# A fused attention and phase-MLP kernel: two groups' phase step in halves, and the whole written-out order replaced

## The chip, the cores and the metric

The kernel runs on one core of a Trainium2 chip. The metric is the device time of one execution in microseconds. Before the change it is 210.47 us, the median of three runs (208.16 to 210.56). The profiled execution took 208.09 us, with a span of 206.3 us from the first instruction to the last; all times of single instructions are from that one.

## What is computed

Two layers, one after the other. The first is attention inside chunks of 64 positions, for 8 batches, 8 heads, 576 positions and a head width of 64. The second works on x, the attention's result with the heads side by side (8 x 576 x 512):

```
scores = scale * q_c @ k_c^T          (per chunk of 64)
x      = softmax(scores) @ v_c
theta  = x @ w_theta
zr, zi = x * cos(theta), x * sin(theta)
y      = w_tok_r @ zr + w_tok_i @ zi  (over the 576 positions of a batch)
u      = x + y
out    = u + relu(u @ w_ch)
```

Inputs and output are fp32; q, k, v and the weights become fp16 on their way into SBUF (theta's weights on the chip), and products accumulate in fp32.

## The kernel before

**Tiles and groups.** The batches are taken in four pairs, numbered 0 to 3. A pair has 2 x 576 rows, nine tiles of 128 rows, numbered 0 to 8. Five groups of tiles pass through the attention together: A (tiles 0, 1) and B (2, 3) of the pair's first batch, C (5, 6) and D (7, 8) of its second, and M, the middle tile 4, whose two halves of 64 rows come from the two batches.

**The order.** There is no scheduler. The string `ORDER` (lines 18 to 66) lists some 650 steps, and the loop at line 589 emits them one after the other. Each engine takes its own instructions in that order; semaphores between engines follow from the tiles. A step is written kind, then pair and group (or pair and tile), then on TensorE steps the PSUM slot. `H.1C.2` is theta of pair 1, group C, into slot 2. The text writes `H.1C` for it. Whoever moves a step in the list moves it on one engine's queue only, and everything behind it on that queue follows.

**The steps of a group**, with the engine that does each:

- `q`, `k`, `v` (lines 170 to 185): loads from HBM, two DMAs each, issued by GpSimd, which converts to fp16. `lw` loads the token weights, `lc` the channel weights, `lt` (SyncE) theta's weights.
- `T`: 32 transposes of q and k on TensorE (16 for M), and `tq` (VectorE) or `tqa` (ScalarE) to copy them from PSUM.
- `S`: scores; `e`: exponentials on ScalarE; `V0`, `V1`: times v, four heads each, with the sum as a 65th column; `v0`, `v1`: normalization on VectorE, which gives x.
- `X` with `x` (ScalarE) or `xv` (VectorE): x transposed on TensorE and copied; or `Xd` (line 388): one DMA transpose on SyncE instead of both.
- `H` (line 399): theta, eight matmuls on 512 columns for a group of two tiles; `g` (line 415): cos and sin on ScalarE; `z` (line 430): the two products on VectorE. For M, `zm` (line 446) moves two halves by DMA.
- `TW` with `twd`: the token weights transposed, once in the kernel, in four pieces.

**The steps of a tile:** `Y` (line 456): nine matmuls with the token weights (in the first pair also in three pieces `Ya`, `Yb`, `Yc`, for tiles 0 to 3); it needs z of both groups of its batch and of M. `y`: u = x + y on VectorE. `U` with `ua` or `uv`: u transposed on TensorE and copied; or `Ud` (line 497): a DMA transpose on SyncE. `W`: four matmuls with the channel weights; `w`: relu and sum; `st`, `sa`: the stores, from SyncE's queue and in the last pair also from ScalarE's.

**Fillers.** `D` (line 155) is one matmul on a blank tile whose result nobody reads. There are 60; they keep TensorE busy while it would wait.

**Buffers that matter.** PSUM has three slots of two banks ("wide") and two of one bank ("thin", for Y, U, W and fillers). cos and sin have three buffers each, q and k eight, the transposed x three, the transposed u five. SyncE's queue is in order as well: a DMA transpose that waits for its data holds up every store and transpose behind it.

Of the kernel before, what the change touches and what calls it, by code (L numbers as in the profile page):

```python
# [10 lines left out]
FP16 = mybir.dt.float16  # L11
# [4 lines left out]


ORDER = """
lt.00 ones.00 D.00.0 D.00.1 D.00.0 D.00.1 D.00.0 D.00.1 D.00.0 q.0M lw.00 q.0B lw.01
D.00.1 D.00.0 init.00 D.00.1 D.00.0 D.00.1 D.00.0 D.00.1 D.00.0 new.00 D.00.1 D.00.0  # L20
k.0M q.0A D.00.1 TW.00.0 D.00.0 v.0M D.00.1 D.00.0 D.00.1 D.00.0 D.00.1 TW.01.1 new.10
T.0M.2 k.0B tq.0M D.00.0 q.0C D.00.1 S.0M.2 twd.00 k.0A D.00.0 D.00.1 v.0B v.0A e.0M
ct.00 D.00.0 D.00.1 D.00.0 D.00.1 D.00.0 lw.02 V1.0M.0 D.00.1 D.00.0 D.00.1 T.0B.2 k.0C
D.00.0 q.0D D.00.1 twd.01 D.00.0 D.00.1 V0.0M.1 v1.0M D.00.0 v0.0M v.0C D.00.1 D.00.0
tqa.0B X.0M.0 D.00.1 S.0B.1 e.0B T.0A.2 D.00.0 lw.03 xv.0M H.0M.0 q.1M D.00.1 D.00.0
k.0D tq.0A S.0A.1 e.0A V1.0B.2 q.1C D.00.1 V0.0A.1 v1.0B v0.0A D.00.0 D.00.1 V0.0B.2
q.1D v0.0B D.00.0 V1.0A.1 D.00.1 X.0B.2 v1.0A X.0A.1 g.0M T.0C.0 x.0B k.1M xv.0A D.00.0
H.0A.1 g.0A z.0M D.00.1 H.0B.2 g.0B tq.0C z.0A S.0C.0 z.0B TW.03.1 Ya.00.0 v.0D zm.0M
TW.02.2 Yb.00 e.0C Yc.00 lc.00 twd.02 T.0D.0 V0.0C.2 twd.03 V1.0C.1 y.00 Ya.02.1 U.00.0
Yb.02 Yc.02 v1.0C v.1M v0.0C y.02 X.0C.1 T.1M.2 tq.1M tqa.0D S.0D.0 k.1C q.1B ua.00  # L30
Ya.03.0 Yb.03 U.02.1 e.0D xv.0C H.0C.2 q.2M V0.0D.0 v0.0D ua.02 V1.0D.1 v1.0D k.1D q.1A
Yc.03 y.03 S.1M.0 e.1M W.02.1 v.1C g.0C V1.1M.1 X.0D.0 W.00.0 xv.0D H.0D.0 k.2M w.00
k.1B w.02 v.1D v1.1M T.1C.2 v.2M q.2C Ya.01.0 Yb.01 U.03.1 g.0D v.1B V0.1M.1 z.0C tq.1C
q.3M z.0D st.00 T.1D.0 S.1C.2 ua.03 Yc.01 v0.1M k.1A y.01 Y.05.1 y.05 U.01.0 T.2M.1
tqa.1D tq.2M uv.01 S.1D.0 e.1C W.03.1 U.05.0 T.1B.2 e.1D uv.05 V0.1C.1 w.03 V1.1C.0
Y.06.0 W.01.1 st.02 v.1A v1.1C v0.1C q.2A y.06 V1.1D.0 tqa.1B S.2M.2 v1.1D V0.1D.1
Y.08.0 w.01 U.06.1 e.2M v0.1D S.1B.2 y.08 X.1D.0 ua.06 xv.1D X.1C.1 e.1B Y.07.0 T.1A.0
V1.1B.2 y.07 q.2B x.1C X.1M.1 tqa.1A xv.1M v1.1B Y.04.1 S.1A.1 st.03 q.3C k.2C q.2D y.04
V1.2M.2 H.1M.0 new.20 v1.2M U.08.0 e.1A W.05.1 w.05 V0.2M.2 ua.08 U.07.0 g.1M k.2B v0.2M
H.1D.1 k.3C uv.07 U.04.1 g.1D z.1M H.1C.2 ua.04 V1.1A.0 v1.1A V0.1A.1 v0.1A g.1C W.06.0  # L40
W.04.1 st.01 q.3D X.2M.0 x.2M X.1A.1 w.06 T.2C.2 xv.1A T.2B.0 w.04 z.1D tqa.2C z.1C
W.08.0 w.08 H.1A.1 V0.1B.2 tqa.2B g.1A st.05 k.2D zm.1M v.3D k.2A k.3M q.3A W.07.1 w.07
Y.16.0 H.2M.0 st.06 D.00.1 v0.1B y.16 v.2C v.2B X.1B.1 k.3D v.3A xv.1B T.2D.2 g.2M
U.16.0 st.04 uv.16 H.1B.0 st.08 st.07 W.16.1 q.3B z.2M tq.2D w.16 Y.18.0 S.2C.1 S.2D.2
g.1B e.2D z.1A T.3M.0 Y.15.1 S.2B.2 z.1B e.2C y.18 y.15 Y.10.0 tqa.3M y.10 V1.2C.1
T.2A.0 v.2A e.2B V1.2B.2 D.00.1 U.10.0 v1.2C Y.13.1 ua.10 v1.2B U.18.0 V0.2C.1 tq.2A
S.2A.2 uv.18 T.3D.0 Y.12.0 y.13 U.13.1 tq.3D v0.2C V0.2B.0 k.3A e.2A V0.2A.2 S.3D.1 v.2D
y.12 ua.13 U.12.0 v0.2B W.10.1 w.10 k.3B ua.12 W.13.0 w.13 W.18.1 st.16 w.18 Y.14.0
T.3C.0 v.3M e.3D T.3A.1 v0.2A U.15.1 V1.2D.2 y.14 st.10 v1.2D Y.11.0 tqa.3C V0.2D.0
st.18 v0.2D ua.15 T.3B.2 tq.3A st.13 Y.17.1 X.2C.0 y.11 S.3A.1 tqa.3B xv.2C S.3B.2 e.3B  # L50
W.15.0 V1.2A.0 v1.2A Xd.2A y.17 Ud.14 H.2C.2 e.3A V1.3A.1 X.2D.0 new.30 Ud.11 xv.2D g.2C
W.12.1 H.2D.0 g.2D Xd.2B v1.3A w.15 W.14.0 w.12 z.2C Ud.17 v.3B z.2D v.3C H.2A.1 W.11.1
st.12 w.14 H.2B.2 zm.2M w.11 V1.3D.0 g.2A st.14 z.2A st.15 v1.3D V0.3A.1 v0.3A Y.27.0
st.11 Y.25.1 V0.3D.0 g.2B y.27 Ud.27 S.3C.2 e.3C z.2B y.25 S.3M.1 v0.3D W.17.0 Ud.25
w.17 Y.26.1 e.3M V0.3M.0 st.17 V1.3M.2 V1.3B.1 y.26 v1.3B Xd.3A v0.3M v1.3M Xd.3M Xd.3D
Y.24.0 V0.3B.1 y.24 Ud.24 V0.3C.0 v0.3C V1.3C.2 v1.3C W.25.1 w.25 st.25 Y.23.0 y.23
W.27.1 w.27 Ud.26 Ud.23 st.27 Y.28.0 W.24.1 w.24 H.3A.0 st.24 H.3M.2 Xd.3C W.26.1 y.28
v0.3B Y.22.0 Xd.3B Ud.28 w.26 g.3M y.22 st.26 Y.20.1 y.20 Y.21.0 z.3M Ud.20 y.21 H.3B.1
W.28.1 w.28 g.3B Ud.22 W.23.0 zm.3M W.22.1 w.23 w.22 g.3A z.3A H.3C.2 st.23 H.3D.1 st.28
st.22 Ud.21 W.20.0 g.3C z.3B Y.30.1 w.20 y.30 g.3D Ud.30 Y.32.0 z.3D y.32 Ud.32 Y.33.1  # L60
Y.31.0 z.3C y.33 Y.35.1 st.20 y.31 y.35 Ud.31 W.30.0 w.30 W.32.1 w.32 W.21.0 Ud.33 sa.30
st.32 sa.32 Ud.35 w.21 Y.38.1 y.38 st.21 W.31.0 st.30 w.31 Ud.38 Y.34.1 y.34 st.31
W.33.0 Ud.34 w.33 st.33 Y.36.1 y.36 Ud.36 Y.37.0 y.37 W.35.1 w.35 Ud.37 W.34.0 sa.33
sa.31 w.34 st.35 st.34 sa.35 W.38.1 W.36.0 w.38 w.36 sa.34 st.38 W.37.1 D.00.0 D.00.0
w.37 sa.37 st.36 sa.36 D.00.1 sa.38 st.37 D.00.0
""".split()


# [1 line left out]
def kernel(  # L70
# [11 lines left out]
    nc = tc.nc  # L82
    B, H, S, D = q.shape
    DM = H * D
    CH = 64
    P = 128
    NDB = DM // P
# [10 lines left out]
    GROUPS = {  # L98
        "M": (MID, None, KT * P),
        "A": (0, 0, 0),  # L100
        "B": (2, 0, GT),
        "C": (5, 1, 0),
        "D": (7, 1, GT),
    }
# [14 lines left out]
    tmp = ctx.enter_context(tc.tile_pool(name="tmp", bufs=3))  # L119
# [3 lines left out]
    def psum2(name, slot, dtype=FP32):  # L123
        n = 1024 if dtype == FP32 else 2048
        return wide.tile([P, n], dtype, name=name, tag=f"wide{slot}")

    def psum1(name, slot, dtype=FP32):
        n = 512 if dtype == FP32 else 1024
        return thin.tile([P, n], dtype, name=name, tag=f"thin{slot}")
# [18 lines left out]
    st = {p: {} for p in range(NP)}  # L148
# [230 lines left out]
    def x_copy(p, g, copy):  # L379
        n = 1 if g == "M" else 2  # L380
        psv = st[p].pop(("ps_xT", g))
        xT = tmp.tile([P, 2 * NDB, P], FP16, name="xT")
        st[p]["xT", g] = xT
        copy(  # L384
            out=xT[:, 0 : n * NDB].rearrange("p a (r c) -> p r a c", r=2), in_=psv
        )
# [9 lines left out]

    def theta(p, g, slot):
        j0, bb, s0 = GROUPS[g]  # L400
        n = 1 if bb is None else 2
        xT = st[p].pop(("xT", g))
        ps = psum2("ps_theta", slot)
        for j in range(n):
            for db in range(NDB):
                nc.tensor.matmul(  # L406
                    ps[:, j * DM : j * DM + DM],
                    xT[:, j * NDB + db, :],
                    wtheta16[:, db, :],
                    start=(db == 0),  # L410
                    stop=(db == NDB - 1),
                )
        st[p]["ps_theta", g] = ps

    def trig(p, g):
        n = 1 if g == "M" else 2
        ps = st[p].pop(("ps_theta", g))
        cos = tmp.tile([P, 2, DM], FP16, name="cos16")
        sin = tmp.tile([P, 2, DM], FP16, name="sin16")
        st[p]["trig", g] = cos, sin  # L420
        pin = ps[:, 0 : n * DM]
        nc.scalar.activation(  # L422
            out=cos[:, 0:n].rearrange("p a e -> p (a e)"), in_=pin,
            func=AF.Sin, bias=pihalf, scale=1.0,
        )
        nc.scalar.activation(  # L426
            out=sin[:, 0:n].rearrange("p a e -> p (a e)"), in_=pin, func=AF.Sin
        )

    def phase(p, g):  # L430
        j0, bb, s0 = GROUPS[g]
        cos, sin = st[p].pop(("trig", g))
        x, zr, zi = st[p]["x"], st[p]["zr"], st[p]["zi"]
        if bb is not None:
            nc.vector.tensor_mul(zr[:, j0 : j0 + 2], x[:, j0 : j0 + 2], cos)
            nc.vector.tensor_mul(zi[:, j0 : j0 + 2], x[:, j0 : j0 + 2], sin)
            return
        lo, hi = half
        t = tmp.tile([P, DM], FP16, name="zmid")
        nc.vector.tensor_mul(t[lo], x[lo, j0], sin[lo, 0])  # L440
        nc.vector.tensor_mul(t[hi], x[hi, j0], cos[hi, 0])
        st[p]["zmid"] = t
        nc.vector.tensor_mul(zr[lo, j0], x[lo, j0], cos[lo, 0])
        nc.vector.tensor_mul(zi[hi, j0], x[hi, j0], sin[hi, 0])

# [82 lines left out]
    def store(p, j, queues):  # L528
# [38 lines left out]
        "x": lambda p, g: x_copy(p, g, nc.scalar.copy),  # L567
        "xv": lambda p, g: x_copy(p, g, nc.vector.tensor_copy),
        "H": theta,
        "g": trig,  # L570
        "z": phase,
        "zm": mid_move,
        "D": idle,
        "Y": y,
# [13 lines left out]
    with tc.manual_schedule():  # L588
        for step in ORDER:
            kind, at, *slot = step.split(".")  # L590
            g = int(at[1]) if at[1].isdigit() else at[1]
# [31 lines left out]
```

The softmax here doesn't subtract the row's maximum and nothing guards it: scores larger than these inputs give would overflow.

## Time and profile before

| engine | busy of the 206.3 us | share |
|---|---|---|
| TensorE matmuls | 191.7 (19.1 of it fillers) | 93% |
| VectorE | 127.5 | 62% |
| GpSimd (loads) | 106.3 | 51% |
| ScalarE | 95.0 | 46% |

| DMA | count | size | us to landing, median |
|---|---|---|---|
| loads of q, k, v by GpSimd | 96 | 128 KB | 5.8 to 6.4 |
| the same, middle tile | 24 | 64 KB | 6.2 to 6.3 |
| stores | 72 | 128 KB | 2.5 to 2.6 |
| DMA transposes of u | 21 | 128 x 512 | 2.5 |
| DMA transposes of x | 7 | 128 x 1024 (one half as wide) | 3.4 |

A busy TensorE is not one at work to its peak: ends of matmuls are modelled, and a matmul on 512 columns is listed at about 380 ns while the next starts 216 ns later. So the text takes start-to-start times for TensorE's steps. Idle time of the other engines matters only where TensorE waits for them. The loads go on until GpSimd's last issue at 111 us and land until 119.8 us; the DMA engines move 147 to 220 GB/s in nearly every slice of that time.

### The profile page before, as it was taken

To read this page: it belongs to the slowest core of one execution; us is meant where nothing else is said; L and a number is where in the kernel's file an instruction comes from. 1 tells how busy PE (TensorE), PEld (TensorE's weight loads), DVE (VectorE), ACT (ScalarE), POOL (GpSimd) and SP (SyncE) were. 2 spreads that over 40 slices of the span, in tenths; PEclk is the share of its full clock that TensorE was granted. 3 is DMA by queue.
4 is the path that set the end of the run, shared out by engine and by line. 5 is a ranking of instruction groups with operands and counts; after the bars stand their busy time and mean duration, and the time that the engine had idled before them with its cause. 6 is when DMAs were issued, how large, how long until landed. Compare 5 with 4: busy or idle time off the path is not lost.

```text
span 206.3 us, 6334 instructions
## 1 busy us (share of the span) xinstructions
PE 191.7 (93%) x2770; PEld 95.3 (46%) x2770; DVE 127.5 (62%) x234; ACT 95.0 (46%) x94; POOL 106.3 (51%) x133
## 2 busy tenths in 40 slices
PE   7779789999989999999999999799999989999991
PEld 2334445554654654554465554344544434444430
DVE  0032488857948557969588665867845645844470
ACT  2016468837954679956725349486002077000000
POOL 7989999988999999967988200000000000000000
PEclk9999999999999999999999999999999999999998
DMA  5999999999999999999999922975867859247665
GB/s 191 181 158 154 161 163 177 147 173 154 197 159 180 186 155 180 180 220 198 187 156 147 186 89 53 128 171 113 129 118 151 166 126 157 51 102 176 160 166 134
DMA packets 139546, 31.88 MB, mean 154 GB/s; under 512 B 132224, under 2 KB 134400, under 8 KB 139520
## 3 DMA queue, kind: packets, MB, share of 16 engines
q0 software_dynamic: 114288, 16.02, 116.5%
q1 hardware_dynamic: 24512, 14.30, 30.9%
q10 hardware_dynamic: 720, 1.18, 2.2%
q8 instruction: 21, 0.34, 0.7%
q14 instruction: 5, 0.04, 0.1%
HBM read 33.06 MB, written 9.44 MB: 206 GB/s over the span
## 4 chain that ended last, share of the span: by engine, by line
PE 60%; POOL 17%; DMA 14%; issue 2%; ACT 2%; DVE 1%; SPq 0%; DVEq 0%; ACTq 0%; POOLq 0%
PE ps_y L475 29%; PE ps_uw L512 12%; POOL qk L174 12%; PE ps_theta L406 9%; POOL v L182 4%; DMA wnat<-in_moe_w_tok_i_dram 3%; DMA wch<-in_moe_w_ch_dram 3%; DMA uT<-u 3%; DMA qk<-in_k_dram 3%; PE ps_qkT L262 3%; PE ps_x L341 3%; PE ps_sT L308 2%; PE ps_uT L492 1%; DMA out_dram<-o 1%; POOL wnat L192 1%
## 5 line engine op out<-in xcount | busy, mean ns | idle before, releaser
L475 PEld LDWEIGHTS <-wT 128*128 128x128 f16 (+1 forms) x360 | 30.5, 100 | 34.4 <-issue 1.2
L475 PE MATMUL ps_y<-zr,wT 128*128 128x512 f16 (+1 forms) x180 | 44.3, 381 | 0.0
L475 PE MATMUL ps_y<-zi,wT 128*128 128x512 f16 (+1 forms) x180 | 41.9, 379 | 0.0
L483 DVE TENSOR_TENSOR u<-ps_y,x 128x512 f16<-128x512 f32 x36 | 24.8, 690 | 21.6 <-PE ps_y L475 21.3
L512 PE MATMUL ps_uw<-wch,uT 128*128 128x512 f16 x144 | 35.8, 380 | 2.2 <-DMA uT<-u 2.2
L174 POOL DMA_DIRECT2D qk<-in_q_dram x40 | 34.3, 881 | 3.7 <-issue 1.4
L182 POOL DMA_DIRECT2D v<-in_v_dram x40 | 34.2, 878 | 3.0 <-DMA qk<-in_k_dram 1.1
L422 ACT ACTIVATE cos<-ps_theta,pihalf 128x1024 f16<-128x1024 f32 (+1 forms) x20 | 20.6, 1031 | 31.7 <-PE ps_theta L406 30.2
L174 POOL DMA_DIRECT2D qk<-in_k_dram x40 | 34.3, 879 | 1.7 <-DMA wnat<-in_moe_w_tok_i_dram 0.6
L406 PE MATMUL ps_theta<-wtheta,xT 128*128 128x512 f16 x144 | 34.0, 379 | 0.0
L521 DVE SCALAR_TENSOR_TENSOR o<-ps_uw,u 128x512 f32<-128x512 f32 x36 | 24.6, 689 | 15.0 <-PE ps_uw L512 14.6
L321 ACT ACTIVATE eT<-ps_sT 128x1024 f16<-128x1024 f32 (+1 forms) x20 | 18.5, 938 | 30.0 <-PE ps_sT L308 28.7
L354 DVE TENSOR_TENSOR x<-ps_x,recip 128x512 f16<-128x512 f32 (+1 forms) x40 | 25.5, 638 | 1.4
L512 PEld LDWEIGHTS <-uT 128*128 128x128 f16 x144 | 12.8, 97 | 18.1 <-DMA uT<-u 3.6
L287 ACT COPY qkT<-ps_qkT 128x2048 f16<-128x2048 f16 x9 | 16.7, 1867 | 9.7 <-PE ps_qkT L262 9.5
L406 PEld LDWEIGHTS <-xT 128*128 128x128 f16 x144 | 13.4, 98 | 16.0 <-DVE xT L384 1.1
L157 PE MATMUL ps_idle<-blank 128*128 128x512 f16 x60 | 19.1, 432 | 1.4 <-DVE pihalf L145 1.2
L426 ACT ACTIVATE sin<-ps_theta 128x1024 f16<-128x1024 f32 (+1 forms) x20 | 18.7, 935 | 0.0
L353 DVE RECIPROCAL recip<-ps_x 128x8 f32<-128x8 f32 (+1 forms) x40 | 7.9, 196 | 11.8 <-PE ps_x L341 11.5
L262 PE MATMUL ps_qkT<-id,qk 64*128 64x64 f16 x576 | 12.5, 191 | 1.8 <-DMA qk<-in_k_dram 1.7
L262 PEld LDWEIGHTS <-qk 64*128 64x128 f16 x576 | 10.0, 95 | 5.0 <-DMA qk<-in_k_dram 2.2
L341 PE MATMUL ps_x<-v,eT 64*64 64x65 f16 x576 | 11.1, 196 | 1.1 <-ACT eT L321 0.7
(42 smaller groups left out, 133.5 us busy)
## 6 DMA issues: line engine op xcount, KB each, us to landing
out_dram<-o SPq DMA_DIRECT2D x63, 128.0 KB, 2.5
qk<-in_q_dram POOLq DMA_DIRECT2D x32, 128.0 KB, 6.4
qk<-in_k_dram POOLq DMA_DIRECT2D x32, 128.0 KB, 6.4
v<-in_v_dram POOLq DMA_DIRECT2D x32, 128.0 KB, 5.8
out_dram<-o ACTq DMA_DIRECT2D x9, 128.0 KB, 2.6
theta<-in_moe_w_theta_dram SPq DMA_DIRECT2D x1, 1024.0 KB, 5.3
wnat<-in_moe_w_tok_r_dram POOLq DMA_DIRECT2D x2, 288.0 KB, 6.3
wnat<-in_moe_w_tok_i_dram POOLq DMA_DIRECT2D x2, 288.0 KB, 6.9
```

Of the source, the lines that this page charges most:

```text
L157: nc.tensor.matmul(ps, blank[:, 0:P], blank, start=True, stop=True)
L174: nc.gpsimd.dma_start(nats[p, g][rows, which, r], (q, k)[which][b, :, t0 : t0 + n, :].rearrange("h s d -> s h d"),)
L182: nc.gpsimd.dma_start(v16[rows, slot + r, :, 0:D], v[b, :, t0 : t0 + n, :].rearrange("h s d -> s h d"),)
L262: nc.tensor.transpose(psv[:, r, w, e, j, :], t[half[r], w, j, 2 * e : 2 * e + 2, :].rearrange("s h d -> s (h d)"), id16[half[r], half[r]],)
L354: nc.vector.tensor_tensor(out=st[p]["x"][:, j0 : j0 + n, f * NE * D : (f + 1) * NE * D].rearrange("p c (h d) -> p c h d", h=NE), in0=psv[: ...
L406: nc.tensor.matmul(ps[:, j * DM : j * DM + DM], xT[:, j * NDB + db, :], wtheta16[:, db, :], start=(db == 0), stop=(db == NDB - 1),)
L422: nc.scalar.activation(out=cos[:, 0:n].rearrange("p a e -> p (a e)"), in_=pin, func=AF.Sin, bias=pihalf, scale=1.0,)
L426: nc.scalar.activation(out=sin[:, 0:n].rearrange("p a e -> p (a e)"), in_=pin, func=AF.Sin)
L475: nc.tensor.matmul(ps[rows], wT[:, kt, cols], z[:, jz, :], start=(kt == 0), stop=(kt == 2 * KT),)
L483: nc.vector.tensor_tensor(out=u, in0=st[p].pop(("ps_y", j))[:, 0:DM], in1=st[p]["x"][:, j], op=ALU.add)
L512: nc.tensor.matmul(ps, uT[:, db * P : db * P + P], wch16[:, db, :], start=(db == 0), stop=(db == NDB - 1),)
L521: nc.vector.scalar_tensor_tensor(out=o, in0=st[p].pop(("ps_uw", j)), scalar=0.0, in1=u, op0=ALU.max, op1=ALU.add)
```

## The change

Two things are done. First, theta, cos/sin and the products can be done for one tile of a group: `Ha`, `ga`, `za` for the first and `Hb`, `gb`, `zb` for the second. The half theta goes into a thin PSUM slot of one bank. The new order uses the halves for groups A and B of pair 0 alone, the first two whole groups. There the chain from theta over cos/sin to z is at the start of everything that follows, and a half can go on while the other is still computed.

Second, `ORDER` is replaced whole, with the aim of keeping DMA transposes clear of the loads. The list has the same loads, matmuls and stores. It has 60 fillers as well, but 36 of them stand ahead of the first `TW` (18 before) and 11 at the end (4 before). Of the copies after `T`, 15 are VectorE's and 5 ScalarE's (10 and 10 before); of those after `X`, 3 are VectorE's and 10 ScalarE's (10 and 3 before). One more tile's u is transposed by DMA (22, 21 before) and one less on TensorE.

The diff of the functions, and the head of the list (the rest of it is as new as this part):

```diff
 ORDER = """
-lt.00 ones.00 D.00.0 D.00.1 D.00.0 D.00.1 D.00.0 D.00.1 D.00.0 q.0M lw.00 q.0B lw.01
-D.00.1 D.00.0 init.00 D.00.1 D.00.0 D.00.1 D.00.0 D.00.1 D.00.0 new.00 D.00.1 D.00.0
-k.0M q.0A D.00.1 TW.00.0 D.00.0 v.0M D.00.1 D.00.0 D.00.1 D.00.0 D.00.1 TW.01.1 new.10
...
-H.0A.1 g.0A z.0M D.00.1 H.0B.2 g.0B tq.0C z.0A S.0C.0 z.0B TW.03.1 Ya.00.0 v.0D zm.0M
-TW.02.2 Yb.00 e.0C Yc.00 lc.00 twd.02 T.0D.0 V0.0C.2 twd.03 V1.0C.1 y.00 Ya.02.1 U.00.0
...
+v.0M v.0A q.0C D.00.1 D.00.0 D.00.1 D.00.0 D.00.1 D.00.0 T.0M.1 tq.0M S.0M.2 e.0M TW.01.1
+D.00.0 T.0B.2 twd.00 D.00.1 D.00.0 v.0B D.00.1 T.0A.0 D.00.0 q.0D lw.02 twd.01 D.00.1
+V0.0M.1 tq.0A tqa.0B v0.0M S.0A.2 e.0A V1.0M.0 S.0B.1 v1.0M D.00.0 e.0B X.0M.2 V0.0A.0
+k.0C V1.0A.1 x.0M H.0M.2 new.10 v0.0A v1.0A X.0A.0 xv.0A V1.0B.1 Ha.0A.1 v1.0B V0.0B.0
+g.0M ga.0A v0.0B lw.03 k.0D z.0M Hb.0A.0 v.0C q.1C X.0B.1 TW.02.2 twd.02 gb.0A T.0C.0
+x.0B q.1D Ha.0B.1 zm.0M Hb.0B.0 tq.0C zb.0A za.0A v.0D TW.03.1 ga.0B gb.0B S.0C.2 twd.03
+q.1M T.0D.0 e.0C lc.00 Ya.02.1 zb.0B Ya.03.0 k.1D Yb.02 Yb.03 za.0B Yc.03 y.03 Yc.02
...
 """.split()
...
+    def tiles_of(g, t):
+        j0, bb, s0 = GROUPS[g]
+        return j0 + (t or 0), 1 if bb is None or t is not None else 2
+
+    def theta(p, g, slot, t=None):
+        n = tiles_of(g, t)[1]
+        xT = st[p]["xT", g]
+        ps = psum2("ps_theta", slot) if t is None else psum1("ps_theta1", slot)
...
-                    xT[:, j * NDB + db, :],
+                    xT[:, (j + (t or 0)) * NDB + db, :],
...
-    def phase(p, g):
-        j0, bb, s0 = GROUPS[g]
-        cos, sin = st[p].pop(("trig", g))
+    def phase(p, g, t=None):
+        bb = GROUPS[g][1]
+        j0, n = tiles_of(g, t)
+        cos, sin = st[p].pop(("trig", g, t))
...
-            nc.vector.tensor_mul(zr[:, j0 : j0 + 2], x[:, j0 : j0 + 2], cos)
-            nc.vector.tensor_mul(zi[:, j0 : j0 + 2], x[:, j0 : j0 + 2], sin)
+            nc.vector.tensor_mul(zr[:, j0 : j0 + n], x[:, j0 : j0 + n], cos[:, 0:n])
+            nc.vector.tensor_mul(zi[:, j0 : j0 + n], x[:, j0 : j0 + n], sin[:, 0:n])
...
+        "Ha": lambda p, g, slot: theta(p, g, slot, 0),
+        "Hb": lambda p, g, slot: theta(p, g, slot, 1),
+        "ga": lambda p, g: trig(p, g, 0),
+        "gb": lambda p, g: trig(p, g, 1),
+        "za": lambda p, g: phase(p, g, 0),
+        "zb": lambda p, g: phase(p, g, 1),
```

The loads begin, with the number of DMAs of each in brackets, before: q.0M (2), lw.00 (1), q.0B (2), lw.01 (1), k.0M, q.0A, v.0M, k.0B, q.0C, k.0A, v.0B, v.0A, lw.02, k.0C, q.0D (2 each); after: q.0M (2), q.0B (2), lw.00 (1), q.0A (2), k.0M (2), lw.01 (1), k.0B, k.0A, v.0M, v.0A, q.0C, v.0B, q.0D, lw.02, k.0C (2 each).

## The prediction

> **What bounds the kernel now.** I read the busy time by stages first, for all work and then for the filler matmuls of line 157 alone (columns: stage, its length, busy time of PE, PEld, DVE, ACT and POOL, granted clock, DMA share, GB/s; the second answer has PE and PEld only).
>
> ```profile
> 0.00:34.00 34.00, 28.04 (x458) 13.31 (x460) 13.22 (x28) 13.38 (x13) 31.61 (x45) 1.00 1.89 170
> 34.00:100.00 66.00, 64.73 (x1204) 35.15 (x1202) 48.90 (x94) 47.37 (x48) 60.88 (x73) 1.00 2.23 177
> 126.00:132.00 6.00, 4.62 (x51) 1.93 (x49) 5.05 (x10) 4.98 (x5) 0.00 (x0) 1.00 0.81 98
> 132.00:200.00 68.00, 67.21 (x491) 30.33 (x490) 42.07 (x74) 17.46 (x19) 0.00 (x0) 1.00 0.68 136
> ```
> ```profile
> 0.00:34.00 34.00, 16.98 (x54) 5.24 (x54) 1.00 1.89 170
> ```
>
> From 34 us on TensorE is full: 64.73 of 66 and 67.21 of 68. In the first 34 it is not: of 28.04 busy, 16.98 are fillers. So a better order can gain in two places only, the start and the few holes later. The timeline of TensorE shows those (start, length, work, and in brackets the idle time before it and what ended it):
>
> ```profile
> 25.49 0.32 PE L341 MATMUL ps_x<-v,eT 64*64 64x65 f16 x16 [0.69 <-ACT eT L321]
> 28.53 0.41 PE L372 MATMUL ps_xT<-id,x 64*128 64x64 f16 x16 [0.43 <-DVE x L354]
> 29.73 1.90 PE L406 MATMUL ps_theta<-wtheta,xT 128*128 128x512 f16 x8
> 31.68 1.89 PE L406 MATMUL ps_theta<-wtheta,xT 128*128 128x512 f16 x8
> 59.27 0.29 PE L262 MATMUL ps_qkT<-id,qk 64*128 64x64 f16 x7 [0.88 <-DMA qk<-in_k_dram]
> 131.56 1.04 PE L512 MATMUL ps_uw<-wch,uT 128*128 128x512 f16 x4 [1.38 <-DMA uT<-u]
> 168.30 1.04 PE L512 MATMUL ps_uw<-wch,uT 128*128 128x512 f16 x4 [0.79 <-DMA uT<-u]
> ```
>
> The start hangs on loads and on the chain behind them; TensorE has dense real work from H.0B, at 31.68. Later a load ends one hole (59) and DMA transposes end two (131, 168). With small ones (0.25 at 35.7, 0.10 at 53.6, 0.44 at 104) the holes sum to 3.9 us. SyncE's queue shows why 131 happened:
>
> ```profile
> 126.17 1.34 SPq L393 DMA_TRANSPOSE xT<-x  x1
> 127.63 2.78 SPq L500 DMA_TRANSPOSE uT<-u  x2
> 130.51 1.26 SPq L393 DMA_TRANSPOSE xT<-x  x1
> 131.86 1.24 SPq L500 DMA_TRANSPOSE uT<-u  x1
> ```
>
> Ud.14, wanted by W.14, was queued behind Xd.2A, which waited for the normalization of group A. The last loads were issued by
>
> ```profile
> 111.42 3.52 POOL L182 DMA_DIRECT2D v<-in_v_dram  x4 [0.16 <-issue]
> ```
>
> and landed at 119.8, so even before the change no transpose met a load; it is the queue and the short distance that cost.
>
> **What the skill says.** The Trainium skill, "DMA: Bandwidth & Descriptors", Issuing engines are not separate DMA queues: DMAs of all issuers share the same 16 engines and interleave. The trace agrees: the 64 KB middle moves took up to 5.7 us to land while loads ran and 1.9 at the end. "TensorE: Matmul & The Clock Gate", What's actually happening: the array drops to half clock after about an idle window of 3.4 us, and needs as much work to come back. The trace agrees for the start: 18 fillers took 6.62 us (368 ns each), six later ones 1.47 (245); its clock column, 1.00 throughout, does not show it. "ScalarE: Activation LUTs", What ACT_TABLE_LOAD costs: a load takes 1283 ns; here ten of 1283. In the new order Exp and Sin alternate as often (ten loads), so this costs nothing.
>
> **The change, part by part.**
>
> Halves. Theta of 0A and 0B in two pieces of four matmuls is the same TensorE work (2 x 0.865 for 1.73). ScalarE: a pair cos and sin on 1024 columns is 1117 + 1021 ns, on 512 it is 687 + 589, so halves cost 2 x 1.28 - 2.14 = 0.42 us more per group. VectorE: no half tile is in the trace; bounds are 0.34 (half of the 684 ns of a 1024-column product) and 0.42 (64 rows x 512 columns). I take 0.42: four make 1.68 against 1.37, 0.3 us more per group. What it buys: cos of the first half starts 0.87 us sooner.
>
> Copies. Over the run five q/k transposes' copies go from ScalarE (1.87) to VectorE (1.22) and seven xT copies the other way (0.69 to 1.02): VectorE +6.1 - 4.8, ScalarE -9.4 + 7.1. Both are below 65% busy, so nothing on the path in sum. I laid the new VectorE and ScalarE sequences against TensorE's with the durations of the rows: in the worst stretch (37 to 60 us) VectorE is nearly full, and Y.06 and S.1C come 0.43 and 0.24 us late. I count 0.4.
>
> Start. Loads keep their pace (about 0.88 us an issue, 6 us to land), so the n-th landing moves little. v.0A becomes load 17 and 18, where k.0A was (TensorE waited for that until 21.98), instead of landing at 24.67. k.0C becomes 27 and 28, where q.0D landed at 29.74 and 30.61. In the new TensorE order T.0C stands ahead of Ha.0B and everything behind it waits, so T.0C ends at 30.61 + 0.5 = 31.1 and Ha.0B starts there. Before it, A's chain fits: x.0B is copied by 29.6 (X.0B at 27.5, ScalarE busy with both cos/sin pairs of A until 28.6, then 1.02). Start of dense work: 31.1 against 31.68, gain 0.58. At this point TW.02 is done already (0.87 of work that before lay behind H.0B); two later fillers (0.43) and one U transpose (0.27: transposes by DMA go from 21 to 22) are gone. Gain 1.57. Summed by rows (Y 1.98 each, W 0.90, H 1.73, T 0.57, S 0.375, V 0.25, X 0.29, U 0.27), the work from this point to the last W is 163.6 us before and 162.0 after. Before took 168.4 (31.68 to 200.1): 3.9 of holes and 0.9 of small steps between groups, which I leave as they are. After Ya and Yb, Yc.03 needs za.0B: ga.0B from 32.0, gb.0B from 34.0 (it takes the cos/sin buffer that za.0A frees, behind tq.0C and zb.0A on VectorE) to 35.2, then two products pairs to 36.9; TensorE is there at 36.4, and its fourth matmul first reads the last of them. Late by 0.1.
>
> Loads later. With TensorE dense from 31.1 I set each group's first use against the landing of the same load number: T.1D 1.0 us to spare, T.1C 0.3, T.1B 0.1, V0.1C 0.5 late, T.1A 0.2 late, T.3A 0.4 late, all of pair 2 two to twenty us early. One shift of 0.5 serves all. Before, the same table is late by up to 2.5 (T.2M, V0.2A) and the holes made up for it.
>
> DMA transposes. From the producer's end on TensorE to the consumer's start the new order leaves Ud.14 30 us (before 15), Ud.11 14, Xd.2A 9.1 (before 7.4), Xd.3A 6.7, Ud.22 18.5 (before 8.1). Ready plus 0.8 us, issue and landing take 3.4 to 5.7, so the holes at 131 and 168 (2.2 us) go. Ud.34 at the end has 3.6, as Ud.37 had 3.5. I keep 0.3 for one that queues.
>
> Fillers. 36 of the 60 now stand ahead of TW.00: 12 slow and 24 at 0.22 end at 11.6 us, when the first token weights have long landed (9.05 before, about 9.9 after), but k.0M lands at 13 to 14.5 and hides this. The 11 at the end run beside the last store (2.5 us). No cost.
>
> Sum: end of TensorE 200.1 - 0.58 - 1.57 - 3.87 + (0.5 loads, 0.4 VectorE, 0.1 Yc, 0.3 transposes, 0.5 for what the table does not see) = 195.9. The tail of 6.2 us (last W, store, end) stays. Span 202.1 of 206.3, ratio 0.980; of 210.47 this is **206.2**.
>
> **Rivals.** (A) New waits take the place of the old: the new order has as little room between steps (x.1B and z of pair 0's C and D 0.04 us, y.02 0.07), so it loses the same 4.8 us over its sum: 31.1 + 162.0 + 4.8 = 197.9, gain 2.2, 208.2 us. For it: before, eleven links had under 0.5 us to spare, now thirteen. Against: the big holes were transposes, which now have room. (B) Slower: between 12 and 31 us TensorE loses its fillers, and waits for T.0C ahead of ready work. If it cools, the five theta pieces and the first transposes run at half pace, up to 5 us; or k.0C lands 2 to 3 us later and all behind it with it: 200.1 - 2.2 - 2 + 5 and more, 212 us. Against: gaps there are 0.5 to 1.5 us, well under the window. (C) No new waits at all: 31.1 + 162.0 + 0.9 = 194.0, 204.2 us.
>
> **How the numbers follow.** Forecast 0.45, A 0.30, B 0.13, C 0.12. A quarter of all is the forecast's lower half and with C and a little of A makes 0.42 for faster than 206.3; B's upper part and accidents make 0.13 for slower; 0.45 lies between. Range 203.2 to 211.0: from below C to most of B.
>
> **What would show it.** T.0C ends near 31.1, waiting for k.0C, and Ha.0B starts at once; matmuls of 220 ns there (not 430) rule out cooling. No hole over 0.5 us from a uT or xT landing; q/k/v landings end holes of at most 0.5 near 59 and 106. Last W ends near 196. It is wrong if k.0C lands after 32, if fillers' absence shows as slow matmuls, or if holes from VectorE in 37 to 60 exceed 1 us.

## The result and the profile after

The changed kernel took 202.98 us (median of 4 runs, 202.68 to 203.27), the kernel before 209.37 in the same session (4 runs, 208.16 to 210.56). The ratio is 0.9695, with a 95% interval of 0.9618 to 0.9772: faster by 3%. Two of the four runs before lie near 210.5; against the usual time of that kernel (208.1 to 208.8, see the first experiment) the gain is nearer 5 us than 6.4. The ratios leave out executions over 1.5% above the fastest of the same kernel, so a ratio can differ a little from the quotient of the medians. The profiled executions last 201.2 and 206.3 us. The forecast of 206.2 was 3.2 us too high, and the result lies just below its range (203.2 to 211.0).

By stages, all work of the kernel after (columns as in the prediction: stage, its length, PE, PEld, DVE, ACT, POOL, clock, DMA share, GB/s):

```profile
0.00:34.00 34.00, 29.23 (x521) 14.92 (x521) 15.17 (x34) 16.62 (x20) 32.37 (x45) 1.00 1.91 172
34.00:100.00 66.00, 64.94 (x1206) 34.73 (x1207) 49.21 (x93) 40.85 (x44) 59.85 (x73) 1.00 2.23 173
126.00:132.00 6.00, 6.00 (x151) 3.13 (x138) 5.08 (x12) 2.35 (x3) 0.00 (x0) 1.00 0.35 68
132.00:196.00 64.00, 61.33 (x386) 26.67 (x385) 39.70 (x67) 15.14 (x16) 0.00 (x0) 1.00 0.72 144
```

and the fillers of line 157 alone (PE and PEld):

```profile
0.00:34.00 34.00, 14.42 (x49) 5.11 (x49) 1.00 1.91 172
```

In the first 34 us TensorE does 14.8 us of real work (29.23 - 14.42) where before it did 11.1. The hole at 131 is gone (6.00 of 6). From 132 on the picture is worse than before: 2.67 us idle of 64, against 0.79 of 68.

TensorE's timeline of the kernel after shows the start and the new holes:

```profile
29.77 0.38 PE L262 MATMUL ps_qkT<-id,qk 64*128 64x64 f16 x14 [0.35 <-DMA qk<-in_k_dram]
30.08 1.90 PE L410 MATMUL ps_theta<-wtheta,xT 128*128 128x512 f16 x8
34.08 0.38 PE L262 MATMUL ps_qkT<-id,qk 64*128 64x64 f16 x14 [0.52 <-DMA qk<-in_k_dram]
60.55 0.32 PE L341 MATMUL ps_x<-v,eT 64*64 64x65 f16 x14 [0.78 <-DMA v<-in_v_dram]
140.79 1.90 PE L410 MATMUL ps_theta<-wtheta,xT 128*128 128x512 f16 x8 [0.45 <-DMA xT<-x]
159.25 1.90 PE L517 MATMUL ps_uw<-wch,uT 128*128 128x512 f16 x8 [1.07 <-DMA uT<-u]
171.82 1.04 PE L517 MATMUL ps_uw<-wch,uT 128*128 128x512 f16 x4 [0.54 <-DMA uT<-u]
195.65 1.04 PE L517 MATMUL ps_uw<-wch,uT 128*128 128x512 f16 x4 [0.45 <-DMA uT<-u]
```

T.0C waits for k.0C (landed 29.73), Ha.0B starts at 30.08. From there on, with 0.19 at 69 (V0.1B) and 0.17 at W.33, the holes sum to 4.17 us: three of loads (1.49: T.0D, V0.1C, V0.1B) and five of DMA transposes (2.68: H.3A, W.21, W.22, W.33, W.34). SyncE's queue shows how the two largest holes of transposes arise:

```profile
155.27 1.34 SPq L393 DMA_TRANSPOSE xT<-x  x1
156.70 1.21 SPq L505 DMA_TRANSPOSE uT<-u  x1
158.01 2.46 SPq L543 DMA_DIRECT2D out_dram<-o  x4
160.52 1.35 SPq L393 DMA_TRANSPOSE xT<-x  x1
161.97 1.18 SPq L543 DMA_DIRECT2D out_dram<-o  x2
163.25 1.25 SPq L505 DMA_TRANSPOSE uT<-u  x1
164.59 0.54 SPq L454 DMA_DIRECT2D zr<-zmid  x1
165.23 0.55 SPq L455 DMA_DIRECT2D zi<-zmid  x1
165.82 1.23 SPq L543 DMA_DIRECT2D out_dram<-o  x2
167.15 1.25 SPq L505 DMA_TRANSPOSE uT<-u  x1
```

Ud.21 (156.70) stands behind Xd.3D (155.27) and lands at 159.2, when W.21 starts. Ud.22 (167.15) stands behind Xd.3C, a store, Ud.23, two middle moves and another store, and lands at 171.8.

The tail, from the last W's end (200.1 and 196.5, its start plus the 0.87 us that a W takes from start to start) to the end of the span, fell from 6.2 to 4.74 us. The timeline around the last sum (DVE) and the stores (ACTq, SPq), before:

```profile
197.47 5.75 ACTq L538 DMA_DIRECT2D out_dram<-o  x5
197.88 3.76 SPq L538 DMA_DIRECT2D out_dram<-o  x5
200.46 0.69 DVE L521 SCALAR_TENSOR_TENSOR o<-ps_uw,u 128x512 f32<-128x512 f32 x1 [0.28 <-DMA out_dram<-o]
```

and after:

```profile
192.95 4.99 ACTq L543 DMA_DIRECT2D out_dram<-o  x5
193.74 4.17 SPq L543 DMA_DIRECT2D out_dram<-o  x5
196.72 0.69 DVE L526 SCALAR_TENSOR_TENSOR o<-ps_uw,u 128x512 f32<-128x512 f32 x1 [0.80 <-PE ps_uw L517]
```

Before, ScalarE's queue goes on until 203.22, 2.1 us after the last sum (201.15): sa.37 waits for that sum, and sa.36 and sa.38, whose data were ready, stand behind it. They land at 203.85, 204.55 and 205.21. After, both queues are empty 0.5 us after the last sum (197.41), and the last two stores land at 199.82 and 200.15.

### The profile page after: what moved, and what is told of

Same layout as the page of the kernel before. It is cut to its first block, busy times and chain, and to the rows that moved or that the text cites. A ratio compares the mean times of both kernels' runs of the same rounds, so it can differ in the third digit from the quotient of the medians.

```text
span 201.2 us, 6347 instructions
## 1 busy us (share of the span) xinstructions
PE 190.9 (95%) x2766; PEld 95.1 (47%) x2766; DVE 127.8 (63%) x235; ACT 93.1 (46%) x100; POOL 106.3 (53%) x133
## 4 chain that ended last, share of the span: by engine, by line
PE 56%; DMA 22%; POOL 18%; issue 3%; DVE 0%; SPq 0%; POOLq 0%
PE ps_y L480 24%; PE ps_uw L517 12%; POOL qk L174 11%; PE ps_theta L410 10%; DMA v<-in_v_dram 7%; DMA uT<-u 6%; POOL v L182 4%; DMA qk<-in_q_dram 4%; DMA qk<-in_k_dram 3%; PE ps_qkT L262 2%; PE ps_x L341 2%; PE ps_sT L308 2%; DMA xT<-x 2%; POOL wnat L192 1%; PE ps_idle L157 1%
## 5 line engine op out<-in xcount | busy, mean ns | idle before, releaser
L517 PE MATMUL ps_uw<-wch,uT 128*128 128x512 f16 x144 | 36.4, 380 | 2.2 <-DMA uT<-u 2.2
L426 ACT ACTIVATE cos<-ps_theta,pihalf 128x1024 f16<-128x1024 f32 (+1 forms) x22 | 21.1, 961 | 26.2 <-PE ps_theta L410 23.2
L157 PE MATMUL ps_idle<-blank 128*128 128x512 f16 x60 | 17.3, 435 | 1.3 <-DVE pihalf L145 1.2
L287 DVE COPY qkT<-ps_qkT 128x2048 f16<-128x2048 f16 x11 | 13.4, 1218 | 4.0 <-PE ps_qkT L262 4.0
L353 DVE RECIPROCAL recip<-ps_x 128x8 f32<-128x8 f32 (+1 forms) x40 | 7.9, 197 | 11.1 <-PE ps_x L341 10.9
L341 PE MATMUL ps_x<-v,eT 64*64 64x65 f16 x576 | 11.9, 196 | 2.2 <-DMA v<-in_v_dram 1.6
L262 PE MATMUL ps_qkT<-id,qk 64*128 64x64 f16 x576 | 12.0, 191 | 1.0 <-DMA qk<-in_k_dram 0.9
L341 PEld LDWEIGHTS <-eT 64*64 64x64 f16 x576 | 8.3, 106 | 9.4 <-issue 4.8
```

Source lines behind the costliest of these rows:

```text
L157: nc.tensor.matmul(ps, blank[:, 0:P], blank, start=True, stop=True)
L341: nc.tensor.matmul(psv[half[r], to, h4, :], eT[rows, h % 2, r if n == 2 else 0, h // 2, :], v16[rows, slot + (r if n == 2 else 0), h, 0 : ...
L426: nc.scalar.activation(out=cos[:, 0:n].rearrange("p a e -> p (a e)"), in_=pin, func=AF.Sin, bias=pihalf, scale=1.0,)
L517: nc.tensor.matmul(ps, uT[:, db * P : db * P + P], wch16[:, db, :], start=(db == 0), stop=(db == NDB - 1),)
```

## The experiments

Times are medians; a ratio is to the kernel before, run in the same session on the same chip.

**The kernel before again** (no edit), to see what its time is.

> The kernel before, unchanged, to see its spread: its four runs lay near 208.2 and near 210.5 us, and none between, while the new order's four lie within 0.6. Theory 1: the before order itself has two outcomes (a load that comes late or not, or a slow stretch); then some runs here lie near 210.5 again, and a profile of one shows where the 2.3 us are. Theory 2: the two values belong to chips or sessions; then all runs here agree within 0.5 us. Ratio to itself 1.000 either way.

Measured: 208.33 us (22 runs, 206.98 to 211.26), ratio 1.0009 [0.9986, 1.0032]; span 206.6, tail 6.14. Over the sessions its medians were 208.06 (43 runs), 208.31 (27), 208.78 (11) and 208.38 (11). So 210.47, the median of the three times before, lay about 2 us above its usual time. Theory 2 fails, theory 1 holds in part: the 22 runs lie mostly between 207 and 209.6, two at 211, and of the 43 other runs of this kernel in the session eight are above 209.8. A time near 210.5 comes up now and then; no profile of such a run was kept, so where its 2 us lie is open.

**The kernel before with queue moves alone.** Two transposes go ahead of what held them, and two ready stores ahead of sa.37:

```diff
+Ud.14 Xd.2A            (Ud.14 was behind Xd.2A)
+y.22 Ud.22             (Ud.22 was behind st.26 and Ud.20)
+w.37 sa.38 sa.36 sa.37 (sa.36, sa.38 were behind sa.37)
```

> The before order with four steps moved: the DMA transposes Ud.14 and Ud.22 ahead of the ones they were queued behind, and the last stores sa.36 and sa.38 ahead of sa.37, which waits for the last sum. Theory (holes and tail are a matter of queue order alone): the holes of 1.38 and 0.79 us at 131 and 168 shrink to under 0.3 each, so the last W ends 1.5 to 2.0 us sooner, and the distance from there to the end falls from 6.2 to about 4.9; total gain 2.8 to 3.3 us, ratio 0.985. Rival (each hole is replaced by the next link's wait, since the steps behind have as little room): last W sooner by under 0.7, only the tail gains 1.3, ratio 0.991.

Measured: 204.89 us (6 runs, 203.8 to 207.64), ratio 0.986 [0.9797, 0.9922]. The last W ends at 197.0 (before 200.1; the same kernel run again 200.5) and the tail is 5.02. In its trace the wait at W.14 is gone, and so is the one at W.22:

```profile
126.73 1.04 PE L512 MATMUL ps_uw<-wch,uT 128*128 128x512 f16 x4
127.60 1.89 PE L406 MATMUL ps_theta<-wtheta,xT 128*128 128x512 f16 x8
129.33 1.03 PE L512 MATMUL ps_uw<-wch,uT 128*128 128x512 f16 x4
130.25 1.90 PE L406 MATMUL ps_theta<-wtheta,xT 128*128 128x512 f16 x8
```

The last W comes 3.1 to 3.5 us sooner, more than the 1.5 to 2.0 that the theory allowed. Some of that isn't of the edit: in this profile the load hole at 59 is 0.26 instead of 0.88, and the one at 104 is replaced by 0.22 at 110. By the medians 3.2 us are gained, about half to two thirds of what the change gives (5 to 6.4), with queue positions alone, none of the new order and no halves.

**The kernel before with the new sequence of its first 15 loads.**

```diff
-q.0M lw.00 q.0B lw.01 k.0M q.0A v.0M k.0B q.0C k.0A v.0B v.0A lw.02 k.0C q.0D
+q.0M q.0B lw.00 q.0A k.0M lw.01 k.0B k.0A v.0M v.0A q.0C v.0B q.0D lw.02 k.0C
```

> The before order with only its first fifteen loads in the new sequence (v.0A lands some 3 us sooner, k.0C some 1 us later). Theory (the start is set by the whole new order of loads, matmuls and copies together; TensorE's and VectorE's order of before takes group B first and can't use it): H.0B starts within 0.7 us of 31.68 and the end moves by under 0.7 us, ratio 0.997 to 1.003. Rival (the load order is what brought the start forward): H.0B starts at 30.2 or sooner and the end comes 1.5 us sooner, ratio 0.993.

Measured: 209.53 us (22 runs), ratio 1.007 [1.0046, 1.0095]: slower. H.0B starts at 33.60 instead of 31.68. Its TensorE timeline gives the reason, which neither theory had:

```profile
14.11 0.75 PE L236 MATMUL ps_wT<-id,wnat 128*64 128x128 f16 x20 [1.97 <-DMA wnat<-in_moe_w_tok_i_dram]
14.79 0.41 PE L262 MATMUL ps_qkT<-id,qk 64*128 64x64 f16 x16
```

TW.01 waits for lw.01, now the sixth load group, and T.0M stands behind it: T.0M starts at 14.79 against 12.95, and the chain keeps this 1.9 us up to H.0B. The new order puts TW.01 behind T.0M and S.0M; loads and TensorE order are one change.

**The new order with the old sequence of the first 15 loads** (the diff above, reversed, in the kernel after).

> The new order with the first fifteen loads in the old sequence (q.0M lw.00 q.0B lw.01 k.0M q.0A v.0M k.0B q.0C k.0A v.0B v.0A lw.02 k.0C q.0D): k.0A lands at 22 instead of 18, v.0A at 24.7 instead of 21.8, k.0C at 28.6 instead of 29.7. Theory (the new start is made by loads and TensorE's order together): Ha.0A starts some 3 us later (28.5), Ha.0B 1 to 2 us later, the end 1.5 to 2.5 us later, ratio against the new order 1.008 to 1.012. Rival (the new TensorE order alone makes it, k.0C being the bound): Ha.0B within 0.5 us of 30.1 and the end within 0.5.

Measured: 205.3 us (6 runs), ratio 0.9879 [0.9838, 0.9921]; Ha.0B at 34.04. The unchanged new order in that session: 203.45 (6 runs, 202.19 to 204.59), ratio 0.9788 [0.9735, 0.9841]; it went in for this comparison and for the clock:

> The new order, unchanged, beside the kernel before on the chip of the next three. Theory (the gain is 5.1 us of span: start, two holes, tail; the rest of the recorded gap came from a median of before that lay in its upper tail): median 203.0 to 203.6, about 4.9 us under the median of before, ratio 0.975 to 0.978. Rival (the new order also escapes a slow stretch that before falls into often): ratio 0.970 or below, since before's median would lie near 209.5.

Its 203.45 is 4.9 us under the kernel before of that session (208.31), as its theory had it.

So each half of the pair without the other costs time: 1.2 to 1.5 us for the new loads in the old order, 1.85 us for the old loads in the new one. The 1.85 us are not the landings alone. In the profile with the old loads the clock was half from 19.31 to 26.14:

```profile
20.00:25.00 5.00, 2.97 (x74) 1.77 (x78) 1.83 (x3) 0.59 (x2) 5.00 (x7) 0.50 2.13 166
```

and the mean clock of all six runs was 0.967 to 0.983, against 0.983 to 1.0 of the unchanged order. By the estimate in the last section, 0.56 us for each half-clock stretch, the two or so more stretches that these runs have on average go with about 1.2 of the 1.85 us.

**The new order with the halves undone.**

```diff
-Ha.0A.1 ... ga.0A ... Hb.0A.0 ... gb.0A ... zb.0A za.0A
+H.0A.2 ... g.0A ... z.0A          (group B likewise)
```

> The new order with theta, cos/sin and products of groups A and B of pair 0 whole again (H, g, z in place of Ha, Hb and so on; wide slots 2, 0, 2, 1, 0 for H.0A, TW.02, T.0C, H.0B, TW.03). Theory (the start of dense work is set by the landing of k.0C at 29.7 and of k.0D at 34.0, so the halves buy little): the first Y starts within 0.6 us of 34.4, end later by 0 to 0.7 us against the new order, that is ratio to before 0.970 to 0.974. Rival (the halves are what shortens the start): first Y later by 1.5 us or more, ratio 0.977 or above.

Measured: 203.62 us (6 runs, 203.31 to 205.51), ratio 0.9804 [0.9753, 0.9855], an interval that overlaps both measurements of the new order (0.9695, 0.9788). Undoing the halves moves three other steps to other PSUM slots (TW.02, T.0C, TW.03). By the ratios set beforehand this is the rival's side (0.977 or above), but those took 0.9695 for the new order, and against the rerun's 0.9788 nothing is left of it. The medians differ by 0.2 us (203.45) and 0.6 us (202.98), in different sessions, so what the halves are worth isn't resolved; most of the gain is there without them, 4.4 us below the 208.06 of the session. In its profiled run something else showed. Stages, and H.0A in TensorE's timeline:

```profile
20.00:25.00 5.00, 3.94 (x121) 2.03 (x117) 3.09 (x9) 3.70 (x4) 5.00 (x8) 0.80 2.47 159
25.00:30.00 5.00, 4.58 (x45) 1.83 (x47) 1.49 (x3) 1.18 (x2) 4.75 (x7) 0.52 1.66 178
```
```profile
26.52 3.52 PE L410 MATMUL ps_theta<-wtheta,xT 128*128 128x512 f16 x8 [0.42 <-DVE xT L384]
```

The clock column reads 0.52, and H.0A takes 3.52 us for eight matmuls that take 1.90 elsewhere. The unchanged new order, run again, had the same in its profile:

```profile
20.00:25.00 5.00, 4.23 (x124) 2.46 (x123) 2.73 (x8) 3.81 (x4) 4.62 (x7) 0.61 2.47 158
25.00:30.00 5.00, 4.50 (x74) 1.99 (x72) 2.83 (x8) 2.70 (x5) 4.79 (x7) 0.71 1.68 186
```

Here k.0C had landed at 29.89, close to the 29.73 of the first profile, but Ha.0B started at 31.78, not 30.08. Its last W ended 1.25 us later (197.75). So the prediction's "gaps there are 0.5 to 1.5 us, well under the window" was right about the gaps (1.23 at most) and wrong in what it took from them: TensorE can fall to half clock in this stretch. Before the clock fell, v.0M landed late (20.33, 19.12 in the first profile) and left the gap of 1.23. A late load alone doesn't start Ha.0B late: in the profile of the old kind of tail below, the same up to the last stores, v.0M landed at 20.25, the clock stayed full there, and Ha.0B started at 30.32. So of the 1.7 us about 1.5 go with the clock. Of these two cooled profiles, the one with whole groups has its first Y at 38.01 and the one with halves at 35.39. In a cooled run the halves may thus matter; one profile of each doesn't show it.

**The new order without the fillers** (it leaves out the matmuls of line 157 and nothing else).

```diff
-ones.00 D.00.0 lt.00 D.00.1 D.00.0 ... (all D steps, at the head and the end)
+ones.00 lt.00 ...
```

> The new order with all 60 filler matmuls taken out; the output is the same. In one run with groups whole, the array's clock record showed half speed from 23.0 to 29.8 us although TensorE had no idle time over 1.1 us there, and theta took 3.5 us instead of 1.9. Theory (the fillers hold the clock): without them the records show half clock over most of the first 30 us, theta of M and 0A takes twice as long, the dense work starts 2 to 5 us later, total 205 to 208 us, ratio 0.985 to 1.0. Rival (in the start TensorE waits for loads anyway, so half pace is hidden and only the first dense 3 us run slow): end later by under 1 us, ratio 0.975 to 0.980.

Measured: 206.51 us (20 runs, 204.41 to 209.94), ratio 0.9903 [0.9875, 0.9932], 3 us more than with them. TensorE then does its first work at 10.34 and runs at half pace until 26.2. The total is what the theory said, 205 to 208, but its path isn't: dense work should have started 2 to 5 us later, and in this profile Ha.0B starts at 30.82 and the first Y at 35.17, between those of the two profiles with fillers (30.08 and 34.39, 31.78 and 35.39).

```profile
30.82 1.90 PE L405 MATMUL ps_theta<-wtheta,xT 128*128 128x512 f16 x8 [0.31 <-ACT xT L379]
35.17 1.04 PE L475 MATMUL ps_y<-zr,wT 128*128 128x512 f16 x4
```

So half pace in the start costs 0.7 to 0.8 us here against the first profile with fillers; the rest is hidden behind waits, as the rival said. In this profile, of a run of 207.96, more time goes later: a hole of 2.64 at 63.73 for which the trace names no cause, half clock behind it, to 67.19, and a hole of 1.59 at W.21 (0.80 in the rerun with fillers). That fillers are worth 3 us is measured; how is open. "Fillers ... No cost" is right for their place.

**Nine of the 36 head fillers moved into 19 to 30 us** (behind V0.0M, V1.0M, V0.0A, V1.0A, X.0A and TW.02).

> The new order with nine fillers taken from the 36 at the head and put where TensorE is thin between 19 and 30 us: two after V0.0M, one each after V1.0M, V0.0A, V1.0A and TW.02, three after X.0A. Theory (half clock for 3.4 or 6.8 us around 20 to 29 us, seen in the records of the new order, comes from these thin stretches and costs 1 to 2 us where it falls): no half-clock stretch between 10 and 35 us in the profile, Ha.0B at 30.1 to 30.5 (31.8 in the throttled profile), median 0.5 to 1.3 us under the new order's 203.4, ratio to before 0.972 to 0.976. Rival (the throttling follows the small matmuls and is not cured by nine fillers, or they delay the chain): Ha.0B after 31, median 203.2 or above.

Measured: 203.5 us (6 runs), ratio 0.9748 [0.9702, 0.9795]: no gain that shows; the unchanged new order did not run in that session. The profile had full clock from 5.7 to 203.7 and Ha.0B at 30.29, but T.1A then waits for its load:

```profile
66.52 0.38 PE L262 MATMUL ps_qkT<-id,qk 64*128 64x64 f16 x14 [1.22 <-DMA qk<-in_k_dram]
```

With 0.53 at V0.1B, 0.46 at T.0D and 0.22 at V0.1C, loads make 2.43 us of holes here. In the cooled rerun of the new order, which started 1.5 us later, they made 1.47. So loads take back some of an earlier start. How much isn't settled: the first profile (Ha.0B at 30.08) had 1.49 of such holes and the best kernel below (30.26) has 1.36.

**The new order with transposes moved in SyncE's queue.**

```diff
+Ud.14 Ud.17 Xd.2A      (both were behind Xd.2A)
+Ud.21 Xd.3D            (Xd.3D was ahead)
+w.21 Ud.22 Xd.3C       (Ud.22 was behind Xd.3C, Ud.23, the middle moves, st.24)
+y.33 Ud.37 st.38       (Ud.37 was behind st.38, st.32, st.31 and others)
```

> The new order with six steps moved on SyncE's queue: Ud.14 and Ud.17 ahead of Xd.2A, Xd.3D behind Ud.21, Ud.22 ahead of Xd.3C, Ud.37 ahead of st.38. Theory (each hole in front of H.3A 0.45, W.21 1.07, W.22 0.54, W.33 0.17 and W.34 0.45 us is a transpose that stood behind another step on that queue): these holes fall under 0.2 each and the end comes 1.8 to 2.6 us sooner, ratio 0.989 against the new order. Rival (their waits pass on to the next step): under 0.8 us.

Measured: 202.18 us (6 runs, 200.68 to 203.09), ratio 0.9721 [0.9671, 0.977], 1.3 below the new order in the same session, between theory (1.8 to 2.6) and rival (under 0.8), though the intervals overlap a little. The trace is clearer: none of the five transpose holes is left, as here, where W.24, W.21 and W.28 run without a gap,

```profile
157.43 2.83 PE L517 MATMUL ps_uw<-wch,uT 128*128 128x512 f16 x12
164.72 1.47 PE L410 MATMUL ps_theta<-wtheta,xT 128*128 128x512 f16 x6 [0.79 <-DMA xT<-x]
```

and one new hole of 0.79 appears (and one of 0.14): Xd.3C, now behind Ud.22, is late for H.3C. What is put ahead in the queue delays what it passes.

**Both, the moved fillers and the moved queue.**

> The nine moved fillers together with the six moved steps on SyncE's queue (a_fix, 202.2 us median). Theory (the two gains add, since they lie in different stretches): median 200.9 to 201.7, ratio to before 0.965 to 0.970. Rival (loads bind between 60 and 70 us, V0.1C, T.1A and V0.1B, and take back what the start gains): within 0.4 of 202.2.

Measured: 201.65 us (6 runs, 200.89 to 203.84), ratio 0.9687 [0.9632, 0.9742]; span 199.5, last W ends at 194.54, tail 4.95. It beats the kernel before clearly. Against the moved fillers alone, in the same session, it is 1.85 us faster. Against the changed kernel the medians say about 1.3 us (201.65 to 202.98), in different sessions. It is the best kernel measured.

**The new order with the old kind of tail** (sa.36 and sa.37 moved behind sa.34, so that ready stores wait behind the last).

> The new order with the last three stores of ScalarE's queue in the manner of the old one: sa.36 and sa.37, ready earlier, stand behind sa.34, which waits for the last sum. Theory (the tail shortened because no store waits behind one that is not ready): the last W is at its place, the distance from its end to the end of the span grows from 4.74 to 5.8 to 6.2 us, total 1.1 to 1.5 us later. Rival (the tail is set by the landing of the last store, whichever it is): under 0.5 us.

Measured: 204.91 us (6 runs, 203.65 to 206.73), ratio 0.9818 [0.9779, 0.9858]. Its profile is that of the run of 206.73, so only the tail is read from it: 6.04 us, against 4.66 (rerun) and 4.74 with the new one. ScalarE's queue shows it, next to the last sum:

```profile
195.34 6.51 ACTq L543 DMA_DIRECT2D out_dram<-o  x5
199.09 0.69 DVE L526 SCALAR_TENSOR_TENSOR o<-ps_uw,u 128x512 f32<-128x512 f32 x1 [0.77 <-PE ps_uw L517]
```

The last sum ends at 199.79, the queue at 201.85. The last three stores of ScalarE land at 202.45, 203.23 and 203.88. This is the 1.4 us of the tail, by itself; the ratios of the new order (0.9695 and 0.9788) lie 0.3 to 1.2 points lower, which is no closer measure of it.

**The best kernel with v.1C ahead of q.1A, and q.2C and q.2M behind v.1B**, to take the load holes at 60 to 70.

> The order with moved fillers and moved transposes (201.65 us median), and three load steps moved besides: v.1C ahead of q.1A, q.2C and q.2M behind v.1B, so that what pair 1 needs between 59 and 70 us lands 1 to 3 us sooner and what pair 2 needs at 78 later. Theory (holes before V0.1C, T.1A and V0.1B, 0.9 to 2 us in the last profiles, are loads in the wrong sequence): these fall under 0.3 together, the end comes 0.6 to 1.2 us sooner, median 200.4 to 201.0. Rival (loads bind as a whole there; the wait moves to T.2C or another group): within 0.4 of 201.65.

Measured: 203.6 us (6 runs), ratio 0.9761 [0.9713, 0.981], above the best kernel by about 2 us, in another session. The holes at 60 to 70 went, and came back larger at T.2A:

```profile
92.29 0.20 PE L262 MATMUL ps_qkT<-id,qk 64*128 64x64 f16 x2 [1.67 <-DMA qk<-in_k_dram]
93.13 0.38 PE L262 MATMUL ps_qkT<-id,qk 64*128 64x64 f16 x14 [0.64 <-DMA qk<-in_k_dram]
```

GpSimd's issues of the best kernel with the change, against those of the best kernel, say why:

```profile
80.80 0.88 POOL L182 DMA_DIRECT2D v<-in_v_dram  x1 [0.58 <-DMA qk<-in_q_dram]
82.42 1.75 POOL L182 DMA_DIRECT2D v<-in_v_dram  x2 [0.74 <-DMA v<-in_v_dram]
84.15 1.78 POOL L174 DMA_DIRECT2D qk<-in_k_dram  x2
```
```profile
77.30 3.56 POOL L182 DMA_DIRECT2D v<-in_v_dram  x4
80.76 1.86 POOL L174 DMA_DIRECT2D qk<-in_k_dram  x2
```

k.2A is issued at 84.15 instead of 80.76, behind loads that now wait for older ones to land (2.55 us of such waits from 50 to 85, 0.28 in the best kernel), and lands at 93.08 instead of 89.14. The theory fell: a load put later held up the whole queue behind it.

## Why the prediction missed

Set out by its own sum, profile to profile, the prediction said a span of 202.1 and 201.2 was measured. Most of the miss in time is in one term outside the kernel, the conversion of spans into time. That the spans are so near is partly luck: within the kernel, tail, start and work came out 3.05 us better than forecast and the holes 2.4 us worse. The step that failed there is the room of the DMA transposes, and the tail that was left as it was.

- **"Ratio 0.980; of 210.47 this is 206.2": wrong, 2.3 us, the largest error.** A ratio of two spans was multiplied with a median of three runs. In both profiled executions the device time is 1.8 us above the span (208.09 to 206.3, 203.02 to 201.2). The consistent number was 202.1 + 1.8 = 203.9. The times before, 208.16 and 210.56 at the ends, showed the spread. The profile of 206.3 belonged to a run of 208.09, near the lower end; the kernel before run again gives 208.1 to 208.8.
- **"The tail of 6.2 us stays": wrong, 1.4 us.** It is 4.74. The order of the stores at the end was not read; the moved stores in both kernels (5.02 from 6.14, and 6.04 from 4.7) show that it sets this time.
- **Start, "Ha.0B starts there", at 31.1: mechanism right, 1.0 us too late.** k.0C landed at 29.73 and not 30.61: it was issued 0.3 us sooner than the load of the same number before, and took 5.9 us instead of 6.4. In the second profile of the new order Ha.0B started at 31.78 for a reason that the prediction had set aside, the clock.
- **"0.5 loads": 1.49 measured.** The waits are at T.0D, V0.1C and V0.1B; "V0.1C 0.5 late" (0.78) was named, T.0D was not among those named. The earlier start is not the whole of it: the rerun that started 1.7 us later lost 1.47 to loads, all of it at V0.1C and V0.1B.
- **"0.3 transposes": wrong, 2.68 measured.** That the holes at 131 and 168 go was right. But the room was counted from the producer's end, "9.1", "6.7", "18.5" us, as if a transpose were issued when its data are ready plus 0.8. It is issued when SyncE's queue comes to it: Ud.22 had 18.5 us of room and still landed 0.54 late. Moving those steps in the queue took these holes away, in the new order and (W.14, W.22) in the kernel before, so this is shown.
- **VectorE 0.4 and Yc 0.1: neither wait appeared.** za.0B ended at 35.37, ahead of the 36.9 expected.
- **Work sum 162.0 and small steps 0.9: good.** From Ha.0B to the last W's end 166.4 us less 4.17 of holes is 162.25, so 0.65 below.

The sum closes: 206.2 - 2.3 (conversion) - 1.4 (tail) - 1.0 (start) - 0.65 (work) + 2.4 (holes 4.17 for 1.8) = 203.2, against 202.98.

Of the rivals, A (new waits replace the old) was right about the amount of waiting, 4.17 of new holes for 3.9 of old, and wrong about the time, since start (1.6), work sum (2.25) and tail (1.4) gained about 5.2 us of span. B's cooling is real in some runs; in the one pair of profiles compared it goes with 1.7 us at Ha.0B and 1.25 at the last W, not five. The halves, which the title names, are not what most of the gain comes from: 4.4 us are there without them. The earlier landing of A's loads (k.0A issued at 11.36 instead of 15.11, v.0A at 14.45 instead of 18.58) with a TensorE order fitted to it, and the order of the last stores, are supported by the runs above. Of the 2.25 us of the work sum no run takes the pieces apart.

## What to carry to other kernels

Convert a difference of spans into time by adding it to the times, with the profile's own device time as the base, and not through a ratio to a small median. Read a DMA transpose's room from its place in the issuing queue, and read the last stores too: a store that waits for the last result must stand last in its queue. When a step is moved in an order, the wait can move to the next transfer in line, so look where it went before calling it a gain.

## What the runs showed of the hardware

- **Half clock without an idle window.** The clock records of the profiles have half-clock stretches of 3.41 or 6.83 us. They were in the new order run again (21.07 to 27.89), with the halves undone (22.99 to 29.82), with the old loads (19.31 to 26.14), with moves in SyncE's queue (22.2 to 25.6), in the best kernel (15.58 to 19.0) and in the best kernel with moved loads (16.5 to 19.91). In the 3.41 us before them TensorE was busy 1.82, 2.42, 1.84, 1.84, 2.31 and 2.19 us, mostly in small matmuls with one to four fillers between, and its longest gap from 12 us to there was 1.23. The Trainium skill, "TensorE: Matmul & The Clock Gate", What's actually happening, tells the drop as one after an idle window of about 3.4 us; here thin work was enough, and the measurement decides.
- **Busy time alone doesn't decide it.** The first profile of the changed kernel, at least 2.3 us busy in any 3.41 us of this stretch, had no half clock; nor had the nine moved fillers, with 2.14. But the kernel before with the new loads was busy only 2.04 and 2.03 us in the two spans of 3.41 us from 9.56 to 16.39 and kept the full clock, while 2.42 was not enough with the halves undone. Where the limit lies, and in what measure, isn't settled.
- **What a half-clock stretch costs.** One stretch of 3.41 us makes the mean clock 0.992, two 0.983. Over 46 runs (the changed kernel, its rerun, and the six variants with halves undone, old loads, moved fillers, moved queue, both, and moved loads), each further stretch goes with 0.56 us more within a kernel (standard error 0.19). That is an estimate from times and clocks that go together; no run changes the clock alone.
- **A queue in order costs at the end.** At the end of the kernel before a store of 128 KB takes 0.5 to 0.8 us to issue and lands 2.3 to 2.8 us after its issue began. Three in a queue behind the last sum made the tail 6.0 to 6.2 us; one per queue, 4.7 to 5.0.
- **A transpose beside stores.** Of the 22 transposes of 128x512 in the changed kernel, 15 landed 2.4 to 2.5 us after issue and seven took 2.75 to 4.63. Ud.22, issued after a store and beside four more, took the longest; in the best kernel one took 5.32. That stores are the cause is not shown.
